# A linear-attention and MLP kernel: idle matmuls regrouped at the start, one weight slice loaded whole, one chunk's outputs moved ahead of an output block

## The chip, the cores and the metric

The kernel runs on one core of a Trainium2 chip. The metric is the device time of one execution in microseconds (us). Before the change it took 214.81 us (median of 6 runs, 214.37 to 216.16). The engines of the core have queues of their own: TensorE (PE) multiplies matrices, VectorE (DVE), ScalarE (ACT) and GpSimd (POOL) work elementwise, and SyncE (SP) only issues DMAs here. POOL issues DMAs as well; all loads that convert float32 to bfloat16 go through it.

## The reference

For 4 sequences with 8 heads of 768 positions and 64 dimensions, a decaying linear attention is computed in blocks, and its output goes through an MLP with an exact GELU:

```python
for b in range(nb):
    qb, kb, vb = q[:, :, sl], k[:, :, sl], v[:, :, sl]
    intra = einsum('bhic,bhjc->bhij', qb, kb) * Dmask          # lam**(i-j), lower triangle
    intra = einsum('bhij,bhjd->bhid', intra, vb)
    inter = einsum('bhid,bhde->bhie', qb * lam_pow, kv_state)
    out[:, :, sl] = intra + inter
    kv_state = lam_block * kv_state + einsum('bhsd,bhse->bhde', kb * rev_pow, vb)

x = out.transpose(0, 2, 1, 3).reshape(3072, 512)
h = x @ w_in                                # 512 x 2048
y = (0.5 * h * (1 + erf(h / sqrt(2)))) @ w_out   # 2048 x 512
```

## The kernel before

The 768 positions are cut into 6 chunks of 128 in each of the 4 sequences, 24 chunks in all. Chunk n belongs to sequence n % 4, at place n // 4. The four chunks of one place form a group of 512 rows for the MLP, so there are 6 groups (g = 0 to 5).

A chunk goes through these steps. Its k and q are transposed, for chunks 0 to 7 on PE (`transposes`, L174), where ACT copies kT out and DVE copies qT out with the powers of lam; later chunks use DMA transposes issued on SP (`dma_transposes`, L187), after POOL has scaled q into q_hat (L192). `scores` (L195) multiplies kT and qT, and DVE masks the two halves into sc_m (L204). `outputs` (L241) is `inter` (product with the sequence's state, from chunk 4 on) and `intra` (product of sc_m and v), after which ACT (groups 0 and 1) or DVE copies the result into the group's x (L237, L239). `next_state` (L206) makes the state for the next place, from k decayed on DVE or POOL (L172).

The MLP of a group (`mlp_blocks`, L251) is a list of blocks: 16 blocks of the first product (`mm1`, L258, four matmuls of one 128-column slice of w_in each, then GELU on ACT), and 16 of the second (`mm2`, L273, four matmuls each; the last part of four copies the result out on ACT and stores it from SP). In groups 0 and 1 the first four blocks of the first product take only the rows of three chunks (384 columns), and an extra block of sixteen small matmuls makes up the fourth, so group 0 has 33 blocks, numbered 0 to 32.

All order is written out by hand: each engine carries out its instructions in the order in which the program issues them. The main loop (L451) goes through the groups' blocks; ahead of block i of group g it calls what `visits[g, i]` (L395 and below) lists for the next groups' chunks. Ahead of that loop comes a start, L330 to L359, in which chunks 0 to 3 are worked on without an MLP beside them. `keep_warm(n)` (L322) there issues n matmuls on a zeroed tile whose result is not used.

The loads are all issued on POOL in the order of the code: k of chunk 0, then q0 k1 q1 k2 q2 v1 v2 k3 q3 (L82), then the first 512 columns of w_in in two loads of 256 columns (L99, L100), v of chunk 3, the other 1536 columns of w_in in three loads of 512, four loads of w_out, and then k, q and v of chunks 4 to 9. A load on POOL waits until the load issued eight places before it has landed. From then on POOL alternates between q_hat, decayed k and the next loads. PSUM tiles come from two sets of four banks, "m" for the MLP, the idle matmuls and the first transposes, "sc" for the rest of the attention.

Around the third edit the order on PE is: scores of chunk 6 and output block 31 of group 0, transposes of chunk 7, output block 32 (the last of group 0), outputs of chunk 6, scores of chunk 7, block 0 of group 1, which reads the x of chunks 4 to 6.

Of the kernel before, what the change touches and what calls it, by code (L numbers as in the profile page):

```python
# [15 lines left out]
def kernel(  # L16
# [47 lines left out]
    def load(n, name):  # L64
        raw[n, name] = qkv_pool.tile([128, H, D], BF16, tag=name, name=f"{name}_t")
        nc.gpsimd.dma_start(raw[n, name], chunk_of(name, n))  # L66
# [24 lines left out]
    def load_w_in(lo, hi):  # L91
        f = slice(lo * 128, hi * 128)
        nc.gpsimd.dma_start(w_in_t[:, :, f], w_in_r[:, :, f])
# [2 lines left out]
        f = NK2 // NS  # L96
        nc.gpsimd.dma_start(w_out_t[:, s * f:(s + 1) * f, :], w_out_r[:, s * f:(s + 1) * f, :])

    load_w_in(0, 2)  # L99
    load_w_in(2, 4)  # L100
    load(3, "v")
    for s in range(4, NK2, 4):
        load_w_in(s, s + 4)
# [53 lines left out]
    live = {}  # L157

    def bank(shape, dtype, tag, name):
        return ps.tile(shape, dtype, tag=tag, name=name, bufs=4)  # L160

    def begin(n):
        c = live[n] = Chunk()
        c.n, c.b, c.so = n, n % B, n // B
        c.q, c.k, c.v = (raw.pop((n, name)) for name in "qkv")
        return c
# [7 lines left out]
    def transposes(c, between=lambda: None):  # L174

        t_ps = [bank([128, HP, C], BF16, "m" if c.so == 0 else "sc", "t_ps") for _ in range(2)]
        for dst, src in zip(t_ps, (c.k, c.q)):
            for hp in range(HP):
                nc.tensor.transpose(dst[:, hp, :], src[:, 2 * hp:2 * hp + 2, :], ident)  # L179
            if src is c.k:  # L180
                between()
        c.kT = work_pool.tile([128, HP, C], BF16, tag="kT", name="kT")
        c.qT = work_pool.tile([128, HP, C], BF16, tag="qT", name="qT")
        nc.scalar.copy(c.kT, t_ps[0])  # L184
        nc.vector.tensor_mul(c.qT, t_ps[1], lam_q)  # L185
# [9 lines left out]
    def scores(c):  # L195
        sc_ps = [bank([128, HP, C], F32, "sc", f"sc_ps{hi}") for hi in range(2)]
        for hp in range(HP):
            for hi in range(2):
                p = slice(hi * D, (hi + 1) * D)
                nc.tensor.matmul(sc_ps[hi][:, hp, :], c.kT[p, hp, :], c.qT[p, hp, :], start=True, stop=True)  # L200
        c.sc_m = work_pool.tile([128, HP, 2, C], BF16, tag="sc_m", name="sc_m")
        dmask_r = dmask.rearrange("p (hp hi) i -> p hp hi i", hi=2)
        for hi in range(2):
            nc.vector.tensor_mul(c.sc_m[:, :, hi, :], sc_ps[hi], dmask_r[:, :, hi, :])  # L204
# [18 lines left out]
    def inter(c):  # L223
        c.o_ps = bank([128, HP, C], F32, "sc", "o_ps")
        if c.so > 0:
            for hp in range(HP):
                nc.tensor.matmul(c.o_ps[:, hp, :], states[c.b][:, hp, :], c.qT[:, hp, :],  # L227
                                 start=(hp == 0), stop=False, skip_group_check=True)

    def intra(c):  # L230
        for hp in range(HP):
            for hi in range(2):
                nc.tensor.matmul(c.o_ps[hi * D:(hi + 1) * D, hp, :], c.v[:, 2 * hp + hi, :], c.sc_m[:, hp, hi, :],  # L233
                                 start=(c.so == 0 and hp == 0), stop=True, skip_group_check=True)
        x_o = xT[c.so][:, :, c.b * C:(c.b + 1) * C]
        if c.so < 2:
            nc.scalar.copy(x_o, c.o_ps)  # L237
        else:
            nc.vector.tensor_copy(x_o, c.o_ps)  # L239

    def outputs(c):  # L241
        inter(c)
        intra(c)
# [78 lines left out]
    def keep_warm(n, new=True):  # L322

        if new:
            idle_ps[0] = bank([128, 512], F32, "m", "idle_ps")
        for _ in range(n):
            nc.tensor.matmul(idle_ps[0], idle[:, :128], idle, start=True, stop=True)  # L327
# [1 line left out]

    nc.vector.tensor_mul(dmask, cmask[:, None, :].to_broadcast((128, H, C)),  # L330
                         lam_m[:, :, None].to_broadcast((128, H, C)))
    keep_warm(9)
    raw[0, "v"] = qkv_pool.tile([128, H, D], BF16, tag="v", name="v_t")
    for n in range(M):
        begin(n)
    transposes(live[0], lambda: keep_warm(3, new=False))
    keep_warm(3, new=False)
    scores(live[0])
    late_powers()
    nc.scalar.copy(live[0].v, v_f)  # L340
# [44 lines left out]
    def first_requests():  # L385
# [5 lines left out]
        for n in (2 * M, 2 * M + 1):  # L391
# [11 lines left out]
        (0, 30): [lambda: first_requests()],  # L403
        (0, 31): [lambda: inter(live[4]), lambda: inter(live[5]), lambda: intra(live[4]), lambda: intra(live[5]),
                  lambda: scores(live[6])],
        (0, 32): [lambda: transposes(live[7])],
        (1, 0): [lambda: outputs(live[6]), lambda: scores(live[7])],
        (1, 2): [lambda: outputs(live[7])],
        (1, 5): [lambda: kv(4, 5)],
        (1, 7): [lambda: kv(6, 7)],  # L410
# [76 lines left out]
```

## Time and profile before

| what | value |
|---|---|
| median of 6 runs | 214.81 us (214.37 to 216.16) |
| the profiled execution | 214.45 us |
| its span, first to last instruction | 212.7 us |
| PE busy | 204.9 us (96% of the span) |
| POOL busy | 104.6 us (49%) |
| ACT busy | 87.2 us (41%) |
| DVE busy | 76.3 us (36%) |
| first product with w_in starts | 18.15 us |
| idle matmuls (L327) | 26 in the profile, 10.6 us |
| loads through POOL's queue | 13.51 MB |

The rows shown below come from the page of the profiled execution and from queries of its trace. A row of the timeline gives the start in us from the first instruction, the duration in us, the engine (PEld is PE's weight load, an engine's name with a q its issuing queue), the source line, the operation, the tiles written and read with their shapes, and how many instructions of a kind were merged; a bracket at its end gives the idle time of the engine ahead of it and what ended that. A row of DMA issues gives the tiles, the issuing queue, the number of issues, the size of each, and the median time in us from the start of the issue to the landing. The duration of a matmul is longer than the distance to the next, because they are pipelined.

### The profile page before, as it was taken

To read this page: it belongs to the slowest core of one execution; us is meant where nothing else is said; L and a number is where in the kernel's file an instruction comes from. 1 tells how busy PE (TensorE), PEld (TensorE's weight loads), DVE (VectorE), ACT (ScalarE), POOL (GpSimd) and SP (SyncE) were. 2 spreads that over 40 slices of the span, in tenths; PEclk is the share of its full clock that TensorE was granted. 3 is DMA by queue.
4 is the path that set the end of the run, shared out by engine and by line. 5 is a ranking of instruction groups with operands and counts; after the bars stand their busy time and mean duration, and the time that the engine had idled before them with its cause. 6 is when DMAs were issued, how large, how long until landed. Compare 5 with 4: busy or idle time off the path is not lost.

```text
span 212.7 us, 3513 instructions
## 1 busy us (share of the span) xinstructions
PE 204.9 (96%) x1426; PEld 104.5 (49%) x1452; DVE 76.3 (36%) x122; ACT 87.2 (41%) x152; POOL 104.6 (49%) x118
## 2 busy tenths in 40 slices
PE   7898999999999999999999999999999999999994
PEld 2455544456655445454544454544454544444442
DVE  4487420175395547465610465610424200000000
ACT  5575663326655311446312355412356311566121
POOL 7995333883996986949679493950000000000000
DMA  8999999999999299997999999995200012100112
GB/s 83 141 148 190 206 206 189 155 209 151 138 126 121 51 149 173 145 154 103 134 88 106 116 237 156 120 154 156 96 0 0 3 49 99 49 3 0 49 49 99
DMA packets 101327, 24.48 MB, mean 115 GB/s; under 512 B 93504, under 2 KB 98368, under 8 KB 101312
## 3 DMA queue, kind: packets, MB, share of 16 engines
q0 software_dynamic: 78592, 13.51, 84.3%
q1 hardware_dynamic: 22720, 10.76, 26.1%
q8 instruction: 11, 0.18, 0.4%
q14 instruction: 4, 0.03, 0.1%
HBM read 27.27 MB, written 6.29 MB: 158 GB/s over the span
## 4 chain that ended last, share of the span: by engine, by line
PE 93%; DMA 2%; DVE 2%; issue 1%; ACT 1%; POOLq 0%
PE h_ps L266 39%; PE o_ps L278 37%; PE o_ps L233 3%; PE sc_ps L200 3%; DMA k_t<-in_k_dram 2%; PE t_ps L179 2%; PE kv_ps L212 2%; PE o_ps L227 2%; PE idle_ps L327 2%; PE o_ps L292 2%; DVE sc_m L204 1%; DVE qT L185 1%; ACT o_sb L283 0%; ACT x_t L237 0%; ACT o_sb L296 0%
## 5 line engine op out<-in xcount | busy, mean ns | idle before, releaser
L266 PE MATMUL h_ps<-x_t,w_in_t 128*128 128x512 bf16 (+2 forms) x401 | 86.3, 362 | 1.0 <-ACT x_t L237 0.3
L278 PE MATMUL o_ps<-w_out_t,g_t 128*128 128x512 bf16 x359 | 81.3, 379 | 0.5
L268 ACT ACTIVATE g_t<-h_ps 128x512 bf16<-128x512 f32 (+1 forms) x98 | 57.7, 588 | 44.0 <-PE h_ps L266 43.9
L266 PEld LDWEIGHTS <-w_in_t 128*128 128x128 bf16 x416 | 37.8, 98 | 41.0 <-issue 0.3
L278 PEld LDWEIGHTS <-g_t 128*128 128x128 bf16 x368 | 35.4, 98 | 42.0
L204 DVE TENSOR_TENSOR sc_m<-sc_ps,dmask 128x512 bf16<-128x512 f32 x48 | 30.0, 683 | 45.2 <-PE sc_ps L200 45.2
L283 ACT COPY o_sb<-o_ps 128x512 f32<-128x512 f32 x23 | 13.5, 586 | 63.3 <-PE o_ps L278 51.1
L192 POOL TENSOR_TENSOR q_hat<-q_t,lam_p 128x512 bf16<-128x512 bf16 x16 | 18.0, 1126 | 23.1 <-issue 9.1
L66 POOL DMA_DIRECT2D k_t<-in_k_dram x24 | 22.0, 918 | 5.2 <-DMA w_in_t<-in_moe_w_in_dram 1.7
L66 POOL DMA_DIRECT2D q_t<-in_q_dram x24 | 21.5, 897 | 5.4 <-DMA w_out_t<-in_moe_w_out_dram 3.4
L66 POOL DMA_DIRECT2D v_t<-in_v_dram x23 | 20.8, 905 | 4.0 <-DMA w_in_t<-in_moe_w_in_dram 1.6
L219 DVE TENSOR_TENSOR tmp<-kv_ps,state 128x512 f32<-128x512 f32 x16 | 11.0, 686 | 17.5 <-PE kv_ps L212 17.5
L172 POOL TENSOR_TENSOR k_dec<-k_t,lam_m 128x512 bf16<-128x512 bf16 x16 | 17.2, 1104 | 0.0
L220 DVE TENSOR_TENSOR state<-tmp,lam_blk 128x512 bf16<-128x512 f32 x16 | 12.2, 760 | 0.6
L239 DVE CAST x_t<-o_ps 128x512 bf16<-128x512 f32 x16 | 10.3, 683 | 4.2 <-PE o_ps L233 4.2
L327 PE MATMUL idle_ps<-idle 128*128 128x512 bf16 x26 | 10.6, 527 | 1.2 <-DVE idle L108 1.2
L185 DVE TENSOR_TENSOR qT<-t_ps,lam_q 128x512 bf16<-128x512 bf16 x8 | 5.5, 690 | 16.8 <-PE t_ps L179 16.6
L200 PE MATMUL sc_ps<-qT,kT 64*128 64x128 bf16 x192 | 8.3, 221 | 0.8 <-DVE qT L185 0.6
L233 PE MATMUL o_ps<-sc_m,v_t 128*64 128x128 bf16 x192 | 8.6, 223 | 0.2
L200 PEld LDWEIGHTS <-kT 64*128 64x128 bf16 x192 | 5.8, 95 | 6.1 <-issue 4.2
L233 PEld LDWEIGHTS <-v_t 128*64 128x64 bf16 x192 | 5.9, 109 | 3.2 <-issue 1.6
L184 ACT COPY kT<-t_ps 128x512 bf16<-128x512 bf16 x8 | 4.7, 588 | 6.6 <-PE t_ps L179 6.5
(41 smaller groups left out, 73.0 us busy)
## 6 DMA issues: line engine op xcount, KB each, us to landing
out_dram<-o_sb SPq DMA_DIRECT2D x23, 256.0 KB, 2.3
k_t<-in_k_dram POOLq DMA_DIRECT2D x24, 128.0 KB, 5.0
q_t<-in_q_dram POOLq DMA_DIRECT2D x24, 128.0 KB, 5.6
v_t<-in_v_dram POOLq DMA_DIRECT2D x23, 128.0 KB, 5.7
w_out_t<-in_moe_w_out_dram POOLq DMA_DIRECT2D x4, 512.0 KB, 17.1
w_in_t<-in_moe_w_in_dram POOLq DMA_DIRECT2D x3, 512.0 KB, 11.0
w_in_t<-in_moe_w_in_dram POOLq DMA_DIRECT2D x2, 256.0 KB, 6.5
v_f<-in_v_dram SPq DMA_DIRECT2D x1, 256.0 KB, 3.8
```

The source lines that it names most:

```text
L66: nc.gpsimd.dma_start(raw[n, name], chunk_of(name, n))
L172: eng.tensor_mul(c.k_dec, c.k, lam_m[:, :, None].to_broadcast((128, H, D)))
L192: nc.gpsimd.tensor_mul(q_hat, c.q, lam_p[:, :, None].to_broadcast((128, H, D)))
L200: nc.tensor.matmul(sc_ps[hi][:, hp, :], c.kT[p, hp, :], c.qT[p, hp, :], start=True, stop=True)
L204: nc.vector.tensor_mul(c.sc_m[:, :, hi, :], sc_ps[hi], dmask_r[:, :, hi, :])
L220: nc.vector.tensor_mul(new, tmp, lam_blk)
L233: nc.tensor.matmul(c.o_ps[hi * D:(hi + 1) * D, hp, :], c.v[:, 2 * hp + hi, :], c.sc_m[:, hp, hi, :], start=(c.so == 0 and hp == 0), stop=T ...
L266: nc.tensor.matmul(h_ps[:, f, :], w, x_t[:, ki, lo:hi], start=(ki == 0 and f == 0), stop=(ki == NK1 - 1), skip_group_check=True)
L268: nc.scalar.activation(g_t[:, kf:kf + n_kf, lo:hi], h_ps, ACT.Gelu)
L278: nc.tensor.matmul(om[io], g_t[:, kf, io * C:(io + 1) * C], w_out_t[:, kf, :], start=(kf == 0), stop=(kf == NK2 - 1))
L283: nc.scalar.copy(o_sb, om[io])
L327: nc.tensor.matmul(idle_ps[0], idle[:, :128], idle, start=True, stop=True)
```

## The change

Three places change.

- The first 512 columns of w_in are loaded by one DMA instead of two of 256 columns.
- In the start, `keep_warm` ahead of the first transposes issues 11 instead of 9 matmuls, between k's and q's transposes of chunk 0 it issues 1 instead of 3, and after them 2 instead of 3.
- `outputs(live[6])` moves from the visit ahead of block 0 of group 1 to the visit ahead of block 32 of group 0, behind the transposes of chunk 7. So it stands ahead of the last output block of group 0 on PE; on ACT its copy into x stands ahead of that block's copy out.

```diff
@@ -96,8 +96,7 @@
-    load_w_in(0, 2)
-    load_w_in(2, 4)
+    load_w_in(0, 4)
     load(3, "v")
     for s in range(4, NK2, 4):
         load_w_in(s, s + 4)
@@ -329,12 +328,12 @@
-    keep_warm(9)
+    keep_warm(11)
     raw[0, "v"] = qkv_pool.tile([128, H, D], BF16, tag="v", name="v_t")
     for n in range(M):
         begin(n)
-    transposes(live[0], lambda: keep_warm(3, new=False))
-    keep_warm(3, new=False)
+    transposes(live[0], lambda: keep_warm(1, new=False))
+    keep_warm(2, new=False)
     scores(live[0])
@@ -403,8 +402,8 @@
         (0, 31): [lambda: inter(live[4]), lambda: inter(live[5]), lambda: intra(live[4]), lambda: intra(live[5]),
                   lambda: scores(live[6])],
-        (0, 32): [lambda: transposes(live[7])],
-        (1, 0): [lambda: outputs(live[6]), lambda: scores(live[7])],
+        (0, 32): [lambda: transposes(live[7]), lambda: outputs(live[6])],
+        (1, 0): [lambda: scores(live[7])],
         (1, 2): [lambda: outputs(live[7])],
```

All other lines are the same; below the first place the line numbers of the changed kernel are lower by one.

## The prediction

> **What bounds the kernel now.** I read the chain that ended last first, then the order of time of its first 60 us, then the DMA issues with their time to landing, then who releases whom on POOL and SP. The chain:
>
> ```profile
> PE 93%; DMA 2%; DVE 2%; issue 1%; ACT 1%; POOLq 0%
> ```
>
> TensorE is the bound, and from 18 us on it hardly pauses. So a step is worth something only in the first 18 us, at a place where PE still waits, or where something lies in wait for a PE that comes earlier. The front, in order of time (start, duration, engine, line):
>
> ```profile
> 1.19 4.02 PE L327 MATMUL idle_ps<-idle 128*128 128x512 bf16 x9 [1.19 <-DVE idle L108]
> ...
> 6.07 0.61 PE L179 MATMUL t_ps<-ident,k_t 128*128 128x128 bf16 x4 [0.85 <-DMA k_t<-in_k_dram]
> ...
> 9.60 0.59 PE L200 MATMUL sc_ps<-qT,kT 64*128 64x128 bf16 x8
> ...
> 10.12 0.61 PE L327 MATMUL idle_ps<-idle 128*128 128x512 bf16 x2
> ...
> 18.15 1.47 PE L266 MATMUL h_ps<-x_t,w_in_t 128*128 128x384 bf16 x8
> ...
> 22.14 0.55 PEld L266 LDWEIGHTS <-w_in_t 128*128 128x128 bf16 x4
> ```
>
> An idle matmul costs 0.43 us until about 10 us (9 of them from 1.19 to 5.0) and 0.22 us after it (10.12 to 10.56 for two): PE runs at half its later speed for its first 10 us, though the granted-clock column says 1.00 throughout. L266 at 18.15 is the first product with w_in; at 22.14 come the first weights of its second 512 columns. When these weights land, from queries around single issues (issue start plus time to landing):
>
> ```profile
> q_t<-in_q_dram POOLq DMA_DIRECT2D x1, 128.0 KB, 5.3
> ...
> w_in_t<-in_moe_w_in_dram POOLq DMA_DIRECT2D x1, 256.0 KB, 6.8
> ...
> w_in_t<-in_moe_w_in_dram POOLq DMA_DIRECT2D x1, 512.0 KB, 9.2
> ```
>
> These are q of chunk 3, the second piece of w_in's first slice and the second slice. Issued at 9.65, 11.26 and 12.87, they land at 14.95, 18.0 and 22.1 (the first piece, 10.51 + 6.2, at 16.7). The last meets PE's 22.14: the weights and PE already arrive together. The place of the third edit:
>
> ```profile
> 52.01 0.59 ACT L237 CAST x_t<-o_ps 128x512 bf16<-128x512 f32 x1
> ...
> 52.64 1.46 PE L266 MATMUL h_ps<-x_t,w_in_t 128*128 128x384 bf16 x8 [0.35 <-ACT x_t L237]
> ```
>
> PE waits 0.35 us for chunk 6's copy, which stands behind an output copy on ACT (51.44 to 52.02). Last, a place that the change does not touch, found by asking which later data land only just in time:
>
> ```profile
> 94.34 1.58 POOL L192 TENSOR_TENSOR q_hat<-q_t,lam_p 128x512 bf16<-128x512 bf16 x1 [2.67 <-DMA q_t<-in_q_dram]
> ...
> qT<-q_hat SPq DMA_TRANSPOSE x1, 2.4
> ...
> 98.24 0.65 PE L200 MATMUL sc_ps<-qT,kT 64*128 64x128 bf16 x16
> ```
>
> The transpose of chunk 15's q, issued on SP at 95.95, lands at 98.35. The scores at 98.24 are of chunks 14 and 15, eight matmuls each at 0.03 us a piece; chunk 15's begin at 98.49. No slack is left there either.
>
> **The idle matmuls.** 9 become 11, 3 between the transposes become 1, 3 behind them become 2. The two added ones run to 1.19 + 11 x 0.43 = 5.9, inside the 0.85 us in which PE waited for k (landing at 6.05): they cost nothing while k is not earlier. Between the transposes 2 x 0.43 = 0.85 us go. The q transposes then start at 6.07 + 0.40 + 0.43 = 6.9, and that is also when q lands (issued 2.67, 4.2 to landing, so 6.9): the next thing late. They end near 7.6, qT runs on DVE from 7.7 to 8.4, and the scores start near 8.4 instead of 9.60: the third idle matmul (9.03 to 9.46) no longer stands ahead of them. So 1.2 us are gained at the scores; if the fast clock comes before 7 us, 1.4. This carries on through DVE's masks to the first product with w_in: 18.15 - 1.2 = 16.95. All loads for it are there: k of chunk 3 at 13.7, q at 14.95.
>
> When PE reaches full speed matters less than it did. Before, a run in which that happens at 12 instead of 10 us pays up to 5 idle matmuls and 16 transposes at double price (5 x 0.21 + 16 x 0.05 = 1.9 us), which is the spread of the times before (214.37 to 216.16); afterwards PE has 0.5 us to spare before the weights. The Trainium skill (TensorE: Matmul & The Clock Gate, "What's actually happening") has the clock follow a free-running window of 3.4 us in which PE must be busy, and warns against fitting to a count of cold matmuls; by it the closed gap brings full speed at 4.6 to 8.0 us. No run here shows that yet.
>
> **The first w_in slice.** Two loads of 256 KB become one of 512 KB. On POOL one issue of 0.83 us goes, and later issues move up (each load still waits for the eighth before it, and only v and two slices get another one, landed by then); that is worth nothing by itself, since the weights land 6 to 9 us after their issue. What counts is the transfer time. From q's landing (14.95) to the second piece's (18.02) are 3.07 us; the 512 KB loads behind land at 22.1, 24.6 and 27.2 (13.61 + 11.0, 14.35 + 12.9), 2.5 to 2.6 us each. So I take 2.53, and 0.54 us less on every later landing; bounds 0 (a slice is as slow as its halves) and 0.6. The single slice lands at 14.95 + 2.53 = 17.5, against 16.7 for the first half before: PE, ready at 16.95, waits 0.5 us there with everything queued behind it, and starts at 17.55. Gain at this point 0.6. The second slice lands at 22.1 - 0.54 = 21.56, and PE, there at 21.54, goes on at 21.6: gain 0.54. The third (24.1) and all of w_out have over 0.5 us of slack. v of chunk 3 lands at 18.3 and is wanted at 18.95.
>
> A rule speaks against this edit: the Trainium skill (DMA: Bandwidth & Descriptors, the table at its head) gives 512 B as the size from which a transfer runs at line rate. A half slice already has rows of 1 KB in memory and 512 B in the chip, so by it the merge saves nothing and the sum would be 214.4. The landings (3.07 against 2.53 us for the same bytes) contradict it, and I follow them.
>
> **Outputs of chunk 6.** They move ahead of the last output block of group 0 (4 matmuls, 0.86 us). The chunk's masked scores are ready at 50.44 on DVE; the products with v would come at 50.69, so the new order has 0.25 us to spare. ACT then copies x at 51.2 to 51.8, behind chunk 7's kT (to 51.2), and the output copy follows, 0.7 us later than before; its store stands on SP behind the transposes of chunks 8 and 9, which keep it until 57.3 anyway. PE runs transposes, outputs, output block, scores of chunk 7, and starts the next group at 52.33 by its own steps (0.15 us for each change to 64-row products, one of which is new at 0.1): 0.32 less than 52.64. Bounds 0.2 and 0.42 (the stall whole).
>
> **The sum.** PE comes 0.54 + 0.32 = 0.86 us earlier to 98 us. There it meets chunk 15's qT, whose chain does not know PE: POOL waits for q's load, makes q_hat, decays k, issues the next six loads, waits for them (POOL's idle time at 53.3, 81.7 and 94.3 ends with a landing of q_t each time). That chain starts from the saturated loads, so it moves up by their 0.54. But the stores around 75 to 83 us hang on PE and move up by 0.86: they overtake the loads by 0.32, and share the engines with them about half and half, so 0.16 to 0.18 may be lost. The landing moves up by 0.36 to 0.54, and what PE brings beyond that is waited away. Of later waits none is near: qT of chunk 17 lands 7 us ahead. I take the middle, 0.45. The profiled execution took 214.45 (span 212.7, 1.75 around it), 0.36 below the median of the runs: 214.45 - 0.45 = 214.0, and as the start depends less on the clock I take it for the median too. Against 214.81 that is -0.4%, just inside the 0.5% that a measurement of this kernel can tell from no change.
>
> **Rivals.** *PE keeps all 0.86*: the POOL chain gains more than its loads, as shorter queues would allow; 214.45 - 0.86 = 213.6. Against it: the coincidence of 98.35 and 98.49. *The merge saves nothing*: the slice lands at 18.0, the second at 22.1, chunk 15's qT where it did, and the front is worth nothing; 214.4. For it speaks that the first 512 KB load behind took 3.2 us after v (18.9 to 22.1), not 2.5. *Chunk 15's qT comes later*: transposes on SP land 2.4 to 5.3 us after issue (median 3.6), and this one had the 2.4. With stores and transposes shifted against the loads it may meet one more load: at the median it is 1.2 later, less the 0.45, so 0.75 lost (215.2); at the worst 2.9 - 0.45 = 2.4 lost (216.9). It decides from 0.45 us on.
>
> **Chances.** My case 0.48 (213.85 to 214.15), all 0.86 kept 0.20, no saving 0.17, qT later 0.15. Beyond 0.5% faster means below 213.74: the second case and a part of the first's lower edge, 0.30. Slower means above 215.88: two thirds of the last, 0.10. The rest, 0.60, is within. The range takes in the first three cases with the bounds of their terms, and a little of the last: 213.3 to 214.9.
>
> **What would show it.** Right: scores near 8.4, first w_in product waiting for a DMA near 17.5, second slice landing near 21.6, no wait of PE on x_t near 52, and a new wait of 0.3 to 0.5 us on qT near 97.7. Wrong: the slice landing at 18 or later, scores of chunks 14 and 15 running through, or chunk 15's qT landing after 98.4.

## The result, and the profile after

The changed kernel takes 215.07 us (median of 35 runs, 213.54 to 221.83) against 214.37 us for the kernel before beside it (72 runs, 213.56 to 217.22). The ratio is 1.0012 with a 95% interval of 0.9994 to 1.003: no change that can be measured. The ratio leaves the most disturbed runs out, and here that hides something: in 15 of 36 runs of the changed kernel the granted clock of TensorE lies at 0.992 or lower, and this has a cause in the kernel, found below. Of the kernel before it was so in 2 of the 90 runs that stood beside the experiments. The 21 runs of the changed kernel with a clock of 0.997 or more have a median of 214.22, the 88 such runs of the kernel before one of 214.38; over all its 36 runs the changed kernel has a median of 215.39, 0.5% above 214.37.

The profiled execution is one with a low clock: 221.32 us, span 219.6, mean granted clock 0.984. So it shows the changed kernel at its worst, and it shows well what the change can set off. The chain that ended last, and the rows of PE and of its granted clock in 40 slices of 5.5 us, from the page of the changed kernel:

```profile
PE   7786999999999999399999999999999999999994
...
PEclk9996999999999999969999999999999999999999
...
PE 85%; DMA 7%; POOL 4%; SPq 1%; issue 1%; ACT 0%; POOLq 0%
```

Two slices at clock 6, the fourth and the eighteenth, and ahead of or in each a slice in which PE pauses. The share of DMA in the chain has gone from 2% to 7%. PE's waits, with the total, the number and the longest in us:

```profile
PE sc_ps L199 <- DMA qT<-q_hat: 3.6, 1, 3.6
PE h_ps L265 <- DMA w_in_t<-in_moe_w_in_dram: 1.8, 1, 1.8
```

The wait for `x_t`, 0.35 us before, is gone. Two others have come, for the slice of w_in and for a transposed q. In order of time (start, duration, engine, line, operation; the bracket is the wait ahead and its releaser):

```profile
16.21 0.40 PE L199 MATMUL sc_ps<-qT,kT 64*128 64x128 bf16 x8 [0.56 <-DVE qT L184]
18.43 2.65 PE L265 MATMUL h_ps<-x_t,w_in_t 128*128 128x384 bf16 x8 [1.81 <-DMA w_in_t<-in_moe_w_in_dram]
...
88.79 0.40 PE L199 MATMUL sc_ps<-qT,kT 64*128 64x128 bf16 x8
92.81 0.40 PE L199 MATMUL sc_ps<-qT,kT 64*128 64x128 bf16 x8 [3.62 <-DMA qT<-q_hat]
```

The eight small products of 1.47 us before take 2.65 us here. Busy time by windows tells why (window, length, busy time and number of instructions of PE, PEld, DVE, ACT and POOL, then PE's granted clock, DMA share and GB/s):

```profile
16.00:18.40 2.40, 0.40 (x8) 0.31 (x8) 1.93 (x4) 0.00 (x0) 0.69 (x1) 1.00 1.61 191
18.40:21.90 3.50, 3.47 (x18) 1.57 (x19) 2.78 (x6) 1.19 (x3) 1.64 (x2) 0.52 1.26 206
92.80:97.20 4.40, 4.39 (x19) 1.72 (x20) 1.29 (x2) 1.19 (x2) 4.26 (x5) 0.61 1.09 208
```

Behind each of the two waits PE runs at about half its clock for some 3.4 us (0.61 over 4.4 us is half for 3.4), busy all the time. So each of these waits costs its length and then another 1.6 to 1.8 us: from the first product with w_in to the first one of 512 columns are 5.53 us here and 3.95 us in the profile of the merge alone (below), where the clock stayed; behind 93 us seven matmuls took 0.21 us more each and two others a part of it. A fall of 0.008 in the mean clock over 212 us is the same 1.7 us, and the runs come in these steps: about 1.000, 0.992 (11 runs, 215.70 to 218.54) and 0.984 (4 runs, 220.80 to 221.83).

Where the 6.87 us between the two profiled executions lie (start of a named product in one less its start in the other):

| stretch | after less before |
|---|---|
| up to the first 512-column product (23.96 against 22.14) | +1.82 |
| from there to group 1's first product (30.18 against 30.50) | -0.32 |
| to the scores of chunk 12 | -0.09 |
| scores of chunk 12 to scores of chunk 14 (16.35 against 10.86) | +5.49 |
| the rest | -0.03 |

### The profile page after: what moved, and what is told of

It reads as the page before. It is cut to its first block, busy times and chain, and to the rows that moved or that the text cites. A ratio compares the mean times of both kernels' runs of the same rounds, so it can differ in the third digit from the quotient of the medians.

```text
span 219.6 us, 3510 instructions
## 1 busy us (share of the span) xinstructions
PE 206.3 (94%) x1425; PEld 104.7 (48%) x1451; DVE 78.4 (36%) x122; ACT 87.1 (40%) x152; POOL 102.2 (47%) x117
## 4 chain that ended last, share of the span: by engine, by line
PE 85%; DMA 7%; POOL 4%; SPq 1%; issue 1%; ACT 0%; POOLq 0%
PE h_ps L265 39%; PE o_ps L277 34%; DMA w_in_t<-in_moe_w_in_dram 4%; DMA qT<-q_hat 3%; PE o_ps L232 3%; PE sc_ps L199 3%; PE o_ps L226 2%; PE kv_ps L211 2%; POOL k_t L66 2%; PE o_ps L291 2%; POOL q_t L66 2%; PE t_ps L178 1%; POOL v_t L66 1%; SPq L190 1%; SPq L192 1%
## 5 line engine op out<-in xcount | busy, mean ns | idle before, releaser
L265 PE MATMUL h_ps<-x_t,w_in_t 128*128 128x512 bf16 (+2 forms) x401 | 89.3, 372 | 2.5 <-DMA w_in_t<-in_moe_w_in_dram 1.8
L265 PEld LDWEIGHTS <-w_in_t 128*128 128x128 bf16 x416 | 38.6, 100 | 44.5 <-issue 3.4
L191 POOL TENSOR_TENSOR q_hat<-q_t,lam_p 128x512 bf16<-128x512 bf16 x16 | 16.8, 1051 | 25.2 <-DMA q_t<-in_q_dram 11.7
L219 DVE TENSOR_TENSOR state<-tmp,lam_blk 128x512 bf16<-128x512 f32 x16 | 13.8, 863 | 0.6
L238 DVE CAST x_t<-o_ps 128x512 bf16<-128x512 f32 x16 | 10.3, 682 | 4.2 <-PE o_ps L232 4.2
L199 PEld LDWEIGHTS <-kT 64*128 64x128 bf16 x192 | 5.7, 94 | 10.1 <-issue 7.6
L326 PE MATMUL idle_ps<-idle 128*128 128x512 bf16 x25 | 8.9, 468 | 1.2 <-DVE idle L107 1.2
```

Of the source, the lines that this page charges most:

```text
L191: nc.gpsimd.tensor_mul(q_hat, c.q, lam_p[:, :, None].to_broadcast((128, H, D)))
L219: nc.vector.tensor_mul(new, tmp, lam_blk)
L265: nc.tensor.matmul(h_ps[:, f, :], w, x_t[:, ki, lo:hi], start=(ki == 0 and f == 0), stop=(ki == NK1 - 1), skip_group_check=True)
```

## The experiments

Three theories were held against each other. *The slice*: PE is ready for w_in near 16.6 us, the whole slice lands only near 18 us, PE waits, and in part of the runs this wait takes the clock down. *Chance*: the loss comes from the clock or from the later transposes, whatever the start does. *The second wait*: chunk 13's transposed q comes late because its transposes, behind an output store on SP, meet the loads that POOL has meanwhile issued.

**The edits one by one.** The merge alone:

```diff
-    load_w_in(0, 2)
-    load_w_in(2, 4)
+    load_w_in(0, 4)
```

> The kernel before with the first w_in slice in one load, nothing else. Theory 1: PE is ready at about 18.15 us, the slice lands at 17.5 to 18.4, so the wait is at most 0.3 us and the clock stays up; time 213.9 to 214.5 (second slice lands 0.3 to 0.5 us earlier). Theory 2 (in the form that one load fewer shifts the rhythm of POOL's queue): runs above 216 as frequent as with the change.

Measured: 215.00 us (214.08 to 222.86, 12 runs), ratio 1.0008 (0.9978 to 1.0038). Three of 12 runs fell: 217.53 at a clock of 0.992, 221.25 and 222.86 at 0.984. The merge by itself is enough for the falls, without the regrouped idle matmuls. Theory 1 had expected none here, with PE ready only at 18.15 us and a wait of 0.3 us at most; but in the profiled run PE was ready at 16.7 us, since its clock rose early. That run had no fall, although PE waits there too:

```profile
16.33 0.40 PE L199 MATMUL sc_ps<-qT,kT 64*128 64x128 bf16 x8 [0.57 <-DVE qT L184]
17.71 1.47 PE L265 MATMUL h_ps<-x_t,w_in_t 128*128 128x384 bf16 x8 [0.97 <-DMA w_in_t<-in_moe_w_in_dram]
```

The idle matmuls alone:

```diff
-    keep_warm(9)
+    keep_warm(11)
...
-    transposes(live[0], lambda: keep_warm(3, new=False))
-    keep_warm(3, new=False)
+    transposes(live[0], lambda: keep_warm(1, new=False))
+    keep_warm(2, new=False)
```

> The kernel before with the idle matmuls regrouped, nothing else. Theory 1: PE is ready for w_in near 16.5 us instead of 18.15, first half at 16.7, then waits on v of chunk 3 (18.9) and the second slice (22.1) give the gain back: nothing won by 22 us, time 214.2 to 214.6, but runs with a late start of the fast clock gone. Theory 2: no different from before at all, 214.4.

Measured: 214.32 us (213.40 to 215.73, 12 runs), ratio 0.9993 (0.9964 to 1.0022), no fall. Worth nothing that can be measured.

The outputs of chunk 6 alone:

```diff
-        (0, 32): [lambda: transposes(live[7])],
-        (1, 0): [lambda: outputs(live[6]), lambda: scores(live[7])],
+        (0, 32): [lambda: transposes(live[7]), lambda: outputs(live[6])],
+        (1, 0): [lambda: scores(live[7])],
```

> The kernel before with the outputs of chunk 6 moved, nothing else. Theory 1: from the second w_in slice to the first product of group 1 PE takes 30.18 us instead of 30.50 (as in the earlier runs with the move), the clock stays up, and the time is 0.1 to 0.3 us below before, less where chunk 15's qT lands late. Theory 2 (the move disturbs the later transposes): no gain, and runs above 216 more frequent.

Measured: 214.49 us (213.76 to 217.61, 12 runs), ratio 0.9995 (0.9965 to 1.0025), one fall (217.61). In its profile the 0.32 us are there, and a wait of 1.22 us on chunk 13's qT gives them back. This kernel has the idle matmuls of before, and its start says something on those:

```profile
7.28 0.81 PE L327 MATMUL idle_ps<-idle 128*128 128x512 bf16 x3
8.29 0.40 PE L200 MATMUL sc_ps<-qT,kT 64*128 64x128 bf16 x8 [0.20 <-DVE qT L185]
...
16.33 0.40 PE L200 MATMUL sc_ps<-qT,kT 64*128 64x128 bf16 x8 [0.57 <-DVE qT L185]
16.66 1.47 PE L266 MATMUL h_ps<-x_t,w_in_t 128*128 128x384 bf16 x8
```

Idle matmuls cost 0.22 us here already at 7.3 us, and not only from 10 us on as in the profile before. With that the old grouping brings the first scores at 8.29 and the last at 16.33; the changed kernel has 8.18 and 16.21.

The change with the merge undone:

```diff
-    load_w_in(0, 4)
+    load_w_in(0, 2)
+    load_w_in(2, 4)
```

> The changed kernel with the first w_in slice in two loads again. Theory 1 (the wait for the merged slice puts PE's clock down): the first half lands near 16.7 us, PE ready near 16.5 waits under 0.4 us there, then up to 0.8 us each on v of chunk 3 (18.9) and on the second slice (22.1); no granted clock below 0.99 at the start, time 213.9 to 214.5, and few runs above 215.5. Theory 2 (the loss comes from the transposes of chunks 12 to 15 meeting POOL's loads, whatever the start does): runs above 216 stay as frequent as with the change, with a wait of over 2 us on qT between 75 and 100 us.

Measured: 214.91 us (213.42 to 216.38, 12 runs), ratio 1.0021 (0.999 to 1.0052), no fall in 12 runs, where the change with its 15 of 36 would give 5. The theory of the slice stands in the falls, but the time that it expected, 213.9 to 214.5, is missed: four of the 12 runs took over 215.5 us at a whole clock. In the profiled run PE waits 2.15 us for v of chunk 3, which lands only at 20.30 us.

**The wait at the slice, filled and lengthened.** Six idle matmuls behind the last scores of the start, all else as changed:

```diff
     scores(live[3])
+    keep_warm(6)
```

> The changed kernel with six more idle matmuls between the scores of chunk 3 and the first product with w_in. Theory 1: the slice still lands at 17.5 to 18.4 us, but PE is busy until about 17.8; no fall of the clock at 18 us, and the time gathers at 213.5 to 214.3, with runs above 216 gone or rare. Theory 2: as many runs above 216 as with the change.

Measured: 214.40 us (213.68 to 215.34, 12 runs), ratio 0.9984 (0.9958 to 1.001), no fall. PE is busy up to the landing:

```profile
16.39 0.40 PE L199 MATMUL sc_ps<-qT,kT 64*128 64x128 bf16 x8 [0.57 <-DVE qT L184]
16.72 1.47 PE L326 MATMUL idle_ps<-idle 128*128 128x512 bf16 x6
18.03 1.46 PE L265 MATMUL h_ps<-x_t,w_in_t 128*128 128x384 bf16 x8
20.09 0.41 PE L232 MATMUL o_ps<-sc_m,v_t 128*64 128x128 bf16 x8 [0.59 <-DMA v_t<-in_v_dram]
```

This was the best ratio of all, so the same kernel was run once more, on another chip:

> The changed kernel with six idle matmuls behind the last scores of the start, a second time, for a narrower interval. Theory: no fall of the clock again (0 of 12 the first time; the changed kernel 15 of 36), median 214.0 to 214.5, 0 to 0.3% under before. Rival (the first time was luck): 4 to 6 of 12 runs with a fall, median near 215.

Measured: 215.13 us (214.03 to 218.88, 12 runs), ratio 1.0019 (0.9991 to 1.0047), one fall. The number of falls agrees, 1 in 24 runs now. The time does not: the theory's 214.0 to 214.5 is missed, and this kernel beats neither of the two. The slice landed at 18.52 us in its profile, so that PE still waited 0.66 us for it. The profiled run (215.88 us, clock 1.000) shows the place where the rest was lost, in the timelines of PE and POOL:

```profile
98.70 0.40 PE L199 MATMUL sc_ps<-qT,kT 64*128 64x128 bf16 x8 [0.41 <-DMA qT<-q_hat]
99.93 0.40 PE L199 MATMUL sc_ps<-qT,kT 64*128 64x128 bf16 x8 [0.83 <-DVE sc_m L203]
...
86.32 0.94 POOL L66 DMA_DIRECT2D k_t<-in_k_dram  x1
...
96.31 1.04 POOL L191 TENSOR_TENSOR q_hat<-q_t,lam_p 128x512 bf16<-128x512 bf16 x1 [3.59 <-DMA q_t<-in_q_dram]
```

POOL issues the loads of chunk 14 1.06 us later than in the profile before (85.26), waits for q, and the transposed q of chunks 14 and 15 lands at 98.57 and 99.79. PE waits 0.41 and 0.83 us. DVE is named for the second, but it is the landing at 99.79 that fits the start at 99.93. The run took 1.35 us more than the first profile of the same kernel (214.53), and these two waits are 1.24 of them.

Five idle matmuls, and chunk 3's outputs one block later:

```diff
     scores(live[3])
+    keep_warm(5)
...
-        (0, 2): [lambda: outputs(live[3])],
+        (0, 3): [lambda: outputs(live[3])],
```

> The changed kernel with five idle matmuls ahead of the first product with w_in, and the outputs of chunk 3 one block later, so that v of chunk 3 has 0.65 us more to land. Theory 1: no clock below 0.998, no wait on v, 213.6 to 214.3, median 0.2 to 0.5 us below before: better than both kernels. Theory 2: runs above 216 as with the change.

Measured: 214.27 us (213.85 to 215.68, 12 runs), ratio 1.0007 (0.9992 to 1.0023), no fall, though in the profile PE still waits 0.69 us for the slice. Again no falls and no gain.

The wait made longer, by loading v of chunk 3 ahead of the slice:

```diff
-    load_w_in(0, 4)
     load(3, "v")
+    load_w_in(0, 4)
```

> The changed kernel with v of chunk 3 loaded ahead of the whole first slice, which so lands about 0.9 us later (18.4 to 19.3). Theory 1: PE waits 2 to 2.8 us instead of 1 to 1.9, and the share of runs with a granted clock at or below 0.992 rises from 0.44 to over 0.7; median above 216. Theory 2 (the wait is harmless in itself, the falls of the clock have another cause): share unchanged, median about 0.5 to 0.9 us higher than with the change.

Measured: 222.79 us (213.91 to 224.95, 6 runs); five of the six have a clock of 0.977 to 0.985, the sixth is whole and takes 213.91. The wait is longer than the expected 2 to 2.8 us. From the profile of this kernel, PE's waits and two windows (columns as above):

```profile
PE h_ps L265 <- DMA w_in_t<-in_moe_w_in_dram: 4.4, 1, 4.4
PE sc_ps L199 <- DMA qT<-q_hat: 2.5, 1, 2.5
```

```profile
21.00:24.60 3.60, 3.51 (x17) 1.56 (x18) 0.00 (x0) 1.14 (x3) 1.78 (x2) 0.50 1.24 207
95.00:98.60 3.60, 3.49 (x23) 1.74 (x24) 1.29 (x2) 1.55 (x3) 3.60 (x5) 1.00 0.91 215
```

The clock fell at the wait of 4.4 us and not behind the one of 2.5. Counted over all kernels, falls occur in 30 of 66 runs where the slice is whole and nothing fills the wait (the change 15 of 36, the merge alone 3 of 12, v first 5 of 6, and 7 of 12 in two kernels below), in 7 of 142 where it comes in two pieces (before 2 of 90), and in 1 of 36 where it is whole and idle matmuls fill the wait. Without the three kernels below that make all transposes on PE, which have falls of their own, it is 23 of 54, 5 of 136 and 1 of 36. The theory of chance is out; that of the slice stands.

**Which waits bring the clock down.** Their length does not decide it. Each trace also keeps a record of the granted clock. In the twelve profiles whose record has entries (those of before and of the idle matmuls alone have none) the clock changes only at whole steps of 3.41 us from the first entry, which lies at 4.90 us in the changed kernel and at 4.55 in v first. So these runs can be cut into windows of 3.41 us. Two of the changed kernel, with the columns as above:

```profile
15.15:18.56 3.41, 1.03 (x16) 0.65 (x14) 2.62 (x5) 0.84 (x2) 1.54 (x3) 1.00 1.52 192
18.56:21.97 3.41, 3.41 (x18) 1.53 (x17) 2.62 (x5) 1.26 (x3) 1.64 (x2) 0.50 1.25 205
```

In the first PE was busy for 1.03 us, and the second has half the clock. The windows with the least work for PE, but for the ends of the runs:

| profile | window | PE waits there for | PE busy | clock in the next window |
|---|---|---|---|---|
| v first | 18.20 to 21.62 | the slice (4.40 us) | 0.53 us | 0.50 |
| changed | 90.24 to 93.65 | qT (3.62) | 0.84 | 0.50 |
| changed | 15.15 to 18.56 | the slice (1.81) | 1.03 | 0.50 |
| v first | 14.79 to 18.20 | the slice (the same 4.40) | 1.34 | 0.50 |
| v first | 93.30 to 96.71 | qT (2.48) | 1.60 | 1.00 |
| two pieces | 18.58 to 21.99 | v of chunk 3 (2.15) | 1.65 | 1.00 |
| merge alone | 14.30 to 17.72 | the slice (0.97) | 1.78 | 1.00 |

All 749 windows of the twelve profiles, from the one ahead of the first entry on, fall in line: ten have PE busy for 1.34 us or less and are followed by half the clock (six of them at the end of a run, where PE has nothing left to do), the others have 1.60 us or more and are followed by the whole clock. So what counted was PE's work within one window. The windows begin elsewhere in each execution (a boundary lies at 18.56 us in the changed kernel and at 17.72 in the merge alone), and the same wait can fall into one of them or be shared by two; that fits a wait that costs the clock in only a part of the runs, though the runs without a profile do not show their windows. With idle matmuls in the wait, the windows around the slice have 2.6 us or more in all three profiles.

**The second wait.** The first form of the theory was that a late PE alone makes it. The kernel before, with PE held up by eight idle matmuls:

```diff
     scores(live[3])
+    keep_warm(8)
```

> The kernel before with eight more idle matmuls ahead of the first product with w_in: PE comes 1.7 us later to all that follows, without a wait and without a fall of the clock. Theory 3 (the second wait in the changed kernel's profile, on qT of chunk 13, comes from PE's lateness alone: the stores and so the transposes on SP slip behind POOL's next loads): a wait of over 1 us on qT of chunk 12 or 13 in the profile, a time of 217 or more, and a lower clock in some runs. Rival (it takes a fall of the clock or chance): no such wait, 215.9 to 216.2, clock 0.998 to 1.000.

Measured: 215.74 us (214.53 to 220.16, 10 runs), ratio 1.0056 (1.003 to 1.0083), two falls. In the profile PE comes 1.7 us later and the end 1.6 us later (216.07 against 214.45); chunk 13's qT lands at 88.69, 0.5 us before PE wants it. So lateness does not make the wait every time, and that form of the theory is out. In part of the runs it may: two of the ten, without a profile, took 220.16 us and, at a whole clock, 219.41. What goes with the wait in the profiles is the distance between two issues. From the timelines of SP and POOL, the changed kernel:

```profile
80.17 0.33 SPq L283 DMA_DIRECT2D out_dram<-o_sb  x1
80.61 2.54 SPq L190 DMA_TRANSPOSE kT<-k_t  x1
83.31 1.19 SPq L192 DMA_TRANSPOSE qT<-q_hat  x1
84.60 1.22 SPq L190 DMA_TRANSPOSE kT<-k_t  x1
85.99 1.26 SPq L192 DMA_TRANSPOSE qT<-q_hat  x1
...
82.36 0.94 POOL L66 DMA_DIRECT2D k_t<-in_k_dram  x1
```

and the kernel before:

```profile
78.76 0.33 SPq L284 DMA_DIRECT2D out_dram<-o_sb  x1
79.19 1.28 SPq L191 DMA_TRANSPOSE kT<-k_t  x1
...
83.99 1.19 SPq L193 DMA_TRANSPOSE qT<-q_hat  x1
...
85.26 0.94 POOL L66 DMA_DIRECT2D k_t<-in_k_dram  x1
```

SP's four transposes of chunks 12 and 13 stand behind a store that waits for PE. POOL's six loads of chunks 14 and 15 come behind q_hat of chunk 13, which waits for that chunk's load, and not behind a store. Before, the loads start behind the last of the four transposes; in the changed kernel they start behind the first. Of the 4.32 us by which the distance shrinks, SP's later issue is 1.42 and POOL's earlier loads are 2.90, so PE's lateness is the smaller part. From all profiles, ordered by the distance:

| kernel | kT of chunk 12 issued | loads begin | distance | qT of chunk 13 lands | from the issue |
|---|---|---|---|---|---|
| filled with 6, again | 79.18 | 86.32 | 7.14 | 86.80 | 7.6 |
| before | 79.19 | 85.26 | 6.07 | 86.37 | 7.2 |
| two pieces | 79.54 | 85.61 | 6.07 | 86.73 | 7.2 |
| filled with 5 | 80.34 | 86.41 | 6.07 | 87.41 | 7.1 |
| filled with 6 | 79.29 | 85.35 | 6.06 | 85.73 | 6.4 |
| merge alone | 78.61 | 84.67 | 6.06 | 85.82 | 7.2 |
| idle matmuls alone | 78.28 | 83.74 | 5.46 | 84.98 | 6.7 |
| late by 8 | 80.81 | 85.21 | 4.40 | 88.69 | 7.9 |
| outputs alone | 78.52 | 82.73 | 4.21 | 88.19 | 9.7 |
| changed | 80.61 | 82.36 | 1.75 | 92.68 | 12.1 |
| v first | 83.84 | 82.59 | -1.25 | 94.98 | 11.1 |

From 5.4 us of distance on, the four take 6.4 to 7.6 us; at 4.2 to 4.4 up to 9.7; below 2 us 11 to 12. Five of the distances are 6.06 or 6.07: in these five profiles q_hat of chunk 13 takes 1.2 to 1.5 us on POOL instead of 1.04 and ends 3.6 us behind the issue of chunk 12's kT each time, so POOL is not everywhere free of what moves SP; what holds it there is not shown. The table is a comparison and not yet an experiment, so the DMA transposes of chunks 8 to 23 were taken away and made on PE (with them goes q_hat on POOL; a chunk's transposes are 8 matmuls there, not the 16 that the first expectation names), in the kernel before, in the changed one and in the one with v first:

```diff
     def request(n):
         begin(n)
-        dma_transposes(live[n])
...
+        add(g, a0 - 1, lambda n=n: [transposes(live[m]) for m in (n, n + 1)])
         add(g, a0, lambda n=n: pair_a(n))
...
+        add(g, a1 - 1, lambda n=n: [transposes(live[m]) for m in (n + 2, n + 3)])
         add(g, a1, lambda n=n: pair_a(n + 2))
```

> The kernel before, with the DMA transposes of chunks 8 to 23 replaced by transposes on PE (as for chunks 4 to 7), issued in pairs ahead of the pairs' scores. Nothing is left out. SP then issues only the output stores. By the durations of the start (16 matmuls of a chunk's transposes in about 0.45 us of PE, and its copies on ACT and DVE): 16 x 0.45 = 7.2 us more on PE, and 0 to 4 us of waits on the copies: 221 to 226 us. No wait of PE on a qT or kT that a DMA delivers, in either theory. A fall of the clock in few runs (before: 2 of 62).

> The changed kernel with the same replacement of the DMA transposes; nothing is left out. Its first 40 us are those of the changed kernel. Theory (a wait at the w_in slice in part of the runs brings the clock down; a late PE then lets chunk 13's transposes meet POOL's loads, which makes the second wait and the second fall): a fall of the clock stays, in 0.3 to 0.45 of the runs, each worth about 1.7 us, but no run has two (in the changed kernel 4 of 36 had), as no transpose on SP is left to come late. In undisturbed runs 0.1 to 0.5 us below p_before by the third edit and the earlier start. Rival (the second fall is chance, or comes from another place): runs with two falls about as often as in the changed kernel, 1 in 9, and slower than p_before by the same 5 to 7 us in these.

> The kernel in which v of chunk 3 is loaded ahead of the whole slice, again with the DMA transposes of chunks 8 to 23 made on PE; nothing is left out. With DMA transposes that kernel was 8.5 us over before by its median (7.5 in the profile: about 4.4 up to group 1's first product, with the fall of the clock behind the wait on w_in, and the rest at chunk 13's qT). Theory: only the first part is left, 3.5 to 5 us over the 223.6 of the kernel before with its transposes on PE, so 227 to 229; falls of the clock at the start in nearly all runs. Rival (a late PE loses as much behind 60 us whatever brings qT): 7.5 to 8.5 over it, 231 to 232.

Measured, six runs each: 223.59 us (222.00 to 225.78) for before, two falls; 223.92 (222.84 to 224.98) for the changed kernel, three falls; 224.92 (224.08 to 225.62) for v first, four falls. Each fall is a single one (0.992). For p_after alone that says little, since 1 in 9 of six runs is less than one; but with DMA transposes the kernel with v first had 0.977 to 0.985 in five of six. Undisturbed, the changed kernel was expected 0.1 to 0.5 us below before; its three runs with a whole clock have a median of 223.33 against 223.00 in four of before. The better test is the time: v first was 8.5 us over before by its median and is 1.3 over it here. The rival had said 7.5 to 8.5, the theory 3.5 to 5, so the theory missed as well. Its reason is in the front, where the slice landed at 19.13 in this profile and at 21.05 in the other:

```profile
16.42 0.40 PE L191 MATMUL sc_ps<-qT,kT 64*128 64x128 bf16 x8 [0.35 <-DVE qT L184]
19.18 1.48 PE L257 MATMUL h_ps<-x_t,w_in_t 128*128 128x384 bf16 x8 [2.35 <-DMA w_in_t<-in_moe_w_in_dram]
```

Within the profiles the step is clear: with DMA transposes v first is 4.40 us late at group 1's first product and 7.48 us at the end; without them 1.80 us (53.31 against 51.51) and 2.08 us (224.08 against 222.00). Without the transposes on SP a PE that was 1.80 us late lost 0.28 us more behind the start; PE was less late here and its clock whole, so what becomes of 4.4 us without them is not shown. The changed kernel, too, is without the second wait, but loses 0.9 us near 63 us, where PE waits 1.87 us on an addition of DVE (`tmp`) instead of 0.82; this place exists only in these kernels. That two of six runs of p_before fell, with no wait at the slice in its profile, was expected by nobody and is not explained.

Moving the transposes of chunks 12 and 13 ahead of the stores on SP would change the distance directly and be the plain remedy; no run here shows what it brings.

## Why the prediction was right, and where it was not

The forecast was no change beyond 0.5%, and that is what was measured. Its 214.0 us is near the 214.22 of the runs with a whole clock; the median of 215.07 lies just above its range (to 214.9), by the falls of the clock. Of its steps only some hold, and that the sum came out near is in part luck: the gain of the merge does not exist, the loss that was to eat it lies at another place, and the falls of the clock are not in it.

- **Outputs of chunk 6: right to the digit.** Between the first 512-column product and group 1's first product lie 30.49 to 30.51 us in the five profiles without this edit and 30.18 to 30.19 in the nine with it: 0.32, as summed. It does not reach the end, as predicted, but the wall is another one (below).
- **Idle matmuls: right in this row, wrong as a gain.** The scores came at 8.18, as the step's second case said (1.4 earlier). But the gain of 1.2 was reckoned against a profile of before in which the fast clock came only near 10 us. The kernel with the old grouping and an earlier fast clock (outputs alone) has the same scores at 8.29, and the edit alone measured 0.9993. The step "18.15 - 1.2 = 16.95" took the late start of one execution for that of the kernel. Whether the closed gap brings the clock earlier is not shown: by the first entry of the clock's record, or where there is none by the idle matmuls, it came at 3.8 to 7.6 us in the nine profiles with the new grouping (four of them ahead of the 4.6 us that the prediction gave as the earliest), and with the old one at 4.1, 4.5, 5.0, 10.1 and 10.3. The spread of the times, which the prediction put down to it, stays: 213.40 to 215.73 with this edit alone.
- **The merge: the step that failed.** "I take 2.53, and 0.54 us less on every later landing": from the landing of chunk 3's q to that of the whole slice were 2.55 to 4.29 us in one piece (mean of six profiles 3.43) and 2.89 to 4.02 in two (mean of six 3.20). From the landing of chunk 3's q to that of the second slice were 7.15, 7.32, 6.91, 6.66, 7.45 and 6.61 us with two pieces (before, two pieces, idle alone, outputs alone, late by 8, before with transposes on PE), mean 7.02, and 7.69, 6.96, 7.61, 5.93, 7.91 and 6.70 with one (changed, filled with 6 twice, merge alone, filled with 5, changed with transposes on PE), mean 7.13. No saving is seen: the means differ by 0.11 us the other way, in a scatter of 0.8 and 2.0 us. The rule in the Trainium skill (DMA: Bandwidth & Descriptors, the table at its head), which the prediction set aside for a single pair of landings, agrees with these rows. Landings at the start differ by over 1 us from run to run, so 3.07 against 2.53 was no evidence.
- **The wait at the slice: seen, but too short and at the wrong price.** "The single slice lands at 17.5 ..., PE, ready at 16.95, waits 0.5 us there": the slice lands at 17.66 to 18.80 in the six profiles that have it in its place, and PE is ready at 16.6 to 16.7, so that unfilled it waits 1.0 to 1.8 us. And a wait that opens in front of PE was priced by its length. In 15 of 36 runs the clock fell as well, at 1.6 to 1.8 us each time, and PE then arrives late at 80 us. This is the term that was missing, not only mis-sized.
- **The wall at 98 us: there, but not the one that binds.** In two pieces, merge alone, filled with 6 and filled with 5 the scores of chunk 15 start 0.13 or 0.14 us after its qT lands, so they are released by it, as predicted; but the waits are 0.02 to 0.21 us, and not 0.3 to 0.5. Once the landing came 1.4 us later than in before (filled with 6, again), which is the rival "chunk 15's qT comes later" at its middle price of 1.2. The larger loss sits one pair earlier, at chunk 13. It had 1.2 us of slack in the profile before (86.37 against 87.61), and the prediction does not name it.
- **Rivals.** *The merge saves nothing* (0.17) is what the landings point to, and its 214.4 is 0.2 off the runs with a whole clock. *PE keeps all 0.86* did not happen. That stores and loads share the engines half and half, by which the sum took off 0.16 to 0.18 us, no row here shows.

The Trainium skill (TensorE: Matmul & The Clock Gate, the table under "Why this matters for your kernels") asks for no pause of PE of more than about 3 us. The rows here are harsher: the clock fell at waits of 1.8, 3.6 and 4.4 us, and did not at 1.0, 1.2, 2.15, 2.35 and 2.5 us. The free-running window, of which the same page speaks, is what the clock's record shows, and it need not be idle: in four windows with PE busy for 0.53 to 1.34 of the 3.41 us the work was too little, while 1.60 us was enough.

## What to carry to other kernels

A new wait ahead of TensorE is not priced by its length alone: here it went with half the clock for 3.4 us in 15 of 36 runs, and what counted in the profiles was how long PE worked within one window of 3.41 us. Idle matmuls laid into the wait ended that (1 fall in 36 runs), without a change of the median that can be measured. So add up PE's work around a new wait, and not only the wait. Before an earlier landing is put into a sum, see how far the same landing differs among executions; one profile of before is one draw of it, and of the moment at which the clock rises too. And where two queues with different masters (here SP, held by PE through a store, and POOL, held by its loads) share the DMA engines, look at the order of their issues: the margin was 6 us in the profile before, and 1.4 us lost by the one and 2.9 won by the other went with a transposed q that took 12 us instead of 7.

## What the runs showed of the hardware that was not expected

- The granted clock went from 1.00 to 0.50 for 3.41 us behind a wait of 1.8 us; it changes only at steps of 3.41 us, and is at half behind each window in which PE was busy for 1.34 us or less and whole behind each with 1.60 us or more (749 windows of twelve profiles).
- The granted-clock column does not show the start: it says 1.00 while the idle matmuls come every 0.43 us. The record behind it has no entry there; in the changed kernel its first lies at 4.90 us, and from 4.96 us on the idle matmuls come every 0.22 us.
- The same four DMA transposes take 6.4 to 12.1 us from the first issue to the last landing: up to 7.6 where the six loads begin 5.4 us or more behind the first issue, 11.1 and 12.1 where they begin less than 2 us behind it.
- Landings of the first loads differ by 1.3 us from one execution to the next (q of chunk 3 between 14.09 and 15.35).

What stays open: why the clock fell in 7 of 142 runs of kernels that have no whole slice to wait for, four of them in the kernel before with its transposes on PE and the one held up by eight matmuls. None of these seven runs has a profile; the thinnest window of such a kernel in a profile, but for the ends of the runs, is that of two pieces above, with 1.65 us. Open is also what makes POOL's loads of chunks 14 and 15 begin anywhere from 82.36 to 86.41 us.
